# Shifted copies on GpSimd, and more slots for the ring that holds them, in a four-layer attention kernel

## The chip, the cores and the metric

The kernel runs on one core of a Trainium2 chip. The metric is the device time of one execution in microseconds (us); lower is better. The core has a matrix engine (TensorE, PE in the profile, with its weight loads as PEld), a vector engine (VectorE, DVE), an activation engine (ScalarE, ACT), a general engine (GpSimd, POOL) and a queue that issues DMAs (SyncE, SP). Each works through its own list of instructions in order and waits for the others by semaphores.

## The reference

Four layers run one after the other on x of 2048 tokens by 512 columns, with 32 heads of 16. Layers 0 and 2 (kind A) attend causally within four segments of 512 tokens and add a memory term; layers 1 and 3 (kind B) are plain attention of all 2048 tokens.

```python
def _A_ref(x, wq, wk, wv, wo, beta):
    ...
    for s in range(N):                       # N = 4 segments of 512 tokens
        qs, ks, vs = (q[:, :, s].copy(), k[:, :, s].copy(), v[:, :, s].copy())
        logits = jnp.einsum('bhqd,bhkd->bhqk', qs, ks) * scale + mask
        p = _softmax(logits, axis=-1)
        a_dot = jnp.einsum('bhqk,bhkd->bhqd', p, vs)
        pq = phi(qs)
        num = jnp.einsum('bhld,bhde->bhle', pq, M)
        den = jnp.einsum('bhld,bhd->bhl', pq, z)[..., None] + 1e-06
        o = g * (num / den) + (1.0 - g) * a_dot
        outs.append(o)
        pk = phi(ks)
        M = M + jnp.einsum('bhld,bhle->bhde', pk, vs)
        z = z + jnp.einsum('bhld->bhd', pk)
    ...

def _B_ref(x, wqkv, wo):
    ...
    scores = jnp.einsum('bhqd,bhkd->bhqk', q, k) * Dh ** (-0.5)
    p = _softmax(scores, axis=-1)
    o = jnp.einsum('bhqk,bhkd->bhqd', p, v)
    return (lambda x, *d: x.transpose(*d))(o, 0, 2, 1, 3).reshape(B, S, D) @ wo

x = A_x
x = x + _A_ref(_layernorm(x, axis=-1), A_wq, A_wk, A_wv, A_wo, A_beta)
x = x + _B_ref(_layernorm(x, axis=-1), B_wqkv, B_wo)
x = x + _A_ref(_layernorm(x, axis=-1), A_wq, A_wk, A_wv, A_wo, A_beta)
x = x + _B_ref(_layernorm(x, axis=-1), B_wqkv, B_wo)
```

## The kernel before

**A program that plans itself.** The Python code keeps a list of instructions for each engine (class `Sched`) and, for each, an estimate of when it ends (`estimate`): `sc.t["dve"]` is the time at which VectorE, by this estimate, is done with all that it was given so far. An instruction is given a duration `ns` and a spacing `gap`, which is `ns - 85` unless it is said otherwise. Where and in what order work is put into the lists is decided by these estimates while the program is built; on the chip the lists then run as they are, held together by semaphores alone. Every tensor region has a `Buf` that remembers its last writer and its readers, from which the waits are made.

**Banks of logits.** A group is four heads (every second one of a chunk of 128 columns) with one segment of 512 queries. Its logits are made in banks, each of one head, 128 keys and 512 queries, with a 32-row matmul (`ps<-qm,KB` in the profile; `qm` is the group's masked copy of the queries, made on GpSimd or VectorE at L1161). A group of kind B has 64 banks. A unit (`unit`) is up to three banks next to each other in PSUM. ScalarE takes their exponential in one instruction (L1244, `pT<-ps`, of 1536, 1024 or fewer columns), and the result is multiplied with V by four 128-column matmuls per bank (`ps<-VB,pT`). In layers of kind A, GpSimd blanks the future keys in `pT` (L1259). When all banks of a group are in, VectorE divides by the row sums (`finish`, L1333 and L1345).

**VectorE's exponential.** Some banks of kind B don't go to ScalarE. VectorE reads the logits from PSUM, scales them and stores them as 16-bit integers whose bits, taken as bfloat16, are a coarse exponential (`dx_first`, L900, of one bank or two). Then it makes three copies, each with another constant added (`EXP_D` = 0, 22, 54, 92; `dx_chain`, L946), and the matmuls with V add up all four (`ps<-VB,dxw` and so on): sixteen matmuls for a bank in place of four. Two banks make a pair. A pair takes four slots of a ring, one for the read and one for each copy; a slot holds 1024 columns, in two halves. A slot is free again when the matmuls that read it have been put in the list.

**The ring.** It has nine slots in a tensor of its own (`dxw`), and six more in the second half of KA, QA and VA, which only the first A layer uses. These are added to the list of free slots (`dx_bufs`) in `dx_widen` when the last segment of layer 0 is through; `wide` is set then. They appear in the profile under the names of the tensors that they lie in: `KA<-ps`, `QA<-dxw`, `ps<-VB,VA` are all work of the ring.

**When a pair is begun.** In `compose`, each unit asks `dx_room`, which says no when few banks are left, when a pair is to be begun and fewer than `DXS` = 4 slots are free, or when VectorE's planned time, with 350 ns for each copy that is still to be made, is over `DQ` = 2200 ns past the unit's start. `dx_find` gives no more than a third of a group's banks to VectorE. The copies are two tasks of the background (`task_dx`), taken one step at a time between units, within a credit of VectorE's time.

**Which engine copies.** In `dx_chain` a copy goes to GpSimd when `POOL_ON` isn't zero and, by the plan, GpSimd would be done with it (`POOL_T` after the later of GpSimd's planned time and the end of the pair's read) before VectorE's planned time plus `POOL_ON`. In the kernel before, `POOL_ON` is 0, and all copies are VectorE's.

Of the kernel before, what the change touches and what calls it, by code (L numbers as in the profile page):

```python
# [3 lines left out]
dt = mybir.dt  # L4
# [73 lines left out]
class Sched:  # L78
# [40 lines left out]
    def add(self, eng, fn, reads=(), writes=(), deps=(), name="", banks=(), ns=300, gap=None, tile=None):  # L119
# [53 lines left out]
        for (bk, mode, alloc) in banks:  # L173
            if mode == "w":
                bk.writes.append(op)
            else:
                bk.reads[eng] = op
                bk.last_read_any = op
# [75 lines left out]
class Builder:  # L254
# [10 lines left out]
    CR_A, CR_B, CR_W, CR_LOW, CARRY, CARRY_W, REST, NEAR, SLACK = 1300, 1500, 1400, 2200, 0, 0, 14, 10, 300  # L265
    ALT3, ALT5, GAP, AHEAD, PE_B, PE_A, PE_LOW, LOW, PAIRS, TAKEN, PAIRS2 = 2, 4, 3, 500, 4, 3, 4, 24, 60, 3, 1
    NKS = 6
    DX_T, POOL_T, POOL_ON = 430, 1150, 0
    DQN, TAKEN_N, REST_N, NEAR_N, NEAR_W = 600, 3, 14, 100, 24
    DQ, DXS, PVN, PVLATE, PVWAIT = 2200, 4, 4, 600, 0  # L270
    DMA_STEPS, DMA_LATE = 2, 300
# [9 lines left out]
    def alloc(self):  # L281
        nc = self.nc
        bf, f32 = dt.bfloat16, dt.float32
        sb = nc.alloc_sbuf_tensor
        self.x = sb("x", [P, NT, D], bf)
        self.xn = sb("xn", [P, 2, D], bf)
        self.xT = sb("xT", [P, 2, NCH, 512], bf)
        self.wA = sb("wA", [P, NCH, 3 * D], bf)
        self.wB = sb("wB", [P, NCH, 3 * D], bf)
        self.woA = sb("woA", [P, NCH, D], bf)  # L290
        self.woB = sb("woB", [P, NCH, D], bf)
        self.KB = sb("KB", [P, self.NKS, NCH, 512], bf)
        self.VB = sb("VB", [P, self.NKS, 4, 544], bf)
        self.QB = sb("QB", [P, 4, NCH, 512], bf)
        self.KA = sb("KA", [P, 2, NCH, 512], bf)
        self.QA = sb("QA", [P, 2, NCH, 512], bf)
        self.VA = sb("VA", [P, 2, 4, 544], bf)
        self.phk = sb("phk", [P, 4, 512], bf)
        self.phq = sb("phq", [P, NCH, 512], bf)
        self.amem = sb("amem", [P, 2, 4, 128], bf)  # L300
        self.oT = sb("oT", [P, 2, NCH, 512], bf)
        self.ob = sb("ob", [P, 2, 4, 128], bf)
        self.rd = sb("rd", [P, 2, 16], f32)
        self.pT = sb("pT", [P, self.NPU, 3, 512], bf)
        self.qm = sb("qm", [P, 4, 512], bf)
        self.dxw = sb("dxw", [P, self.NDX, 1024], dt.uint16)
        self.ident = sb("ident", [P, P], bf)
        self.zero = sb("zero", [P, P], bf)
        self.hmask = sb("hmask", [P, 8], f32)
        self.lnst = sb("lnst", [P, 2, 4, 8], f32)  # L310
        self.lnw = sb("lnw", [P, 2, 4, 4], f32)
        self.bet = sb("bet", [P, H], bf)
        self.gtok = sb("gtok", [P, H], f32)
        self.gout = sb("gout", [P, H], f32)
        self.M = sb("M", [P, NCH, 8, 17], f32)
        self.Mn = sb("Mn", [P, NCH, 8, 16], bf)
        self.Mz = sb("Mz", [P, NCH, 8], bf)
        self.rg = sb("rg", [P, 1, 4, H], f32)
        self.ps = nc.alloc_psum_tensor("ps", [P, 4096], f32)
        self.psb = self.ps[:, :].bitcast(bf)  # L320
        self.sems = {e: nc.alloc_semaphore(f"ev_{e}") for e in ENGS}
        self.tsems = [[nc.alloc_semaphore(f"tr{i}"), 0, None] for i in range(8)]
        self.dsems = [nc.alloc_semaphore(f"dma{i}") for i in range(24)]

        B = Buf
        n2 = lambda nm, a, b: [[B(f"{nm}{i}_{j}") for j in range(b)] for i in range(a)]
        n1 = lambda nm, a: [B(f"{nm}{i}") for i in range(a)]
        self.b_x = n1("x", NT)
        self.b_xn = n1("xn", 2)
        self.b_xT = n2("xT", 2, 4)  # L330
        self.b_wA = n1("wA", 3)
        self.b_wB = n1("wB", 1)
        self.b_woA, self.b_woB = B("woA"), B("woB")
        self.b_KB = n2("KB", self.NKS, NCH)
        self.b_VB = n2("VB", self.NKS, 4)
        self.b_QB = n2("QB", 4, NCH)
        self.b_KA = n2("KA", 2, NCH)
        self.b_QA = n2("QA", 2, NCH)
        self.b_VA = n2("VA", 2, 4)
        self.b_phk = n1("phk", 4)  # L340
        self.b_phkc = n1("phkc", NCH)
        self.b_phq = n1("phq", NCH)
        self.b_amem = n1("amem", 2)
        self.b_oT = n2("oT", 2, NCH)
        self.b_ob = n2("ob", 2, 2)
        self.b_rd = n1("rd", 2)
        self.b_pT = n1("pT", self.NPU * 3)
        self.b_qm = n1("qm", 4)
        self.b_dxw = n2("dxw", self.NDX + 6, 2)
        self.b_last = n1("last", 2)  # L350
        self.b_zero = B("zero")
        self.b_ident, self.b_hm = B("ident"), B("hm")
        self.b_lnst = n2("lnst", 2, 4)
        self.b_lnw = n1("lnw", 2)
        self.b_bet, self.b_g, self.b_gout = B("bet"), B("g"), B("gout")
        self.b_M, self.b_Mn, self.b_Mz = n1("M", 2), B("Mn"), B("Mz")
        self.b_rg = n1("rg", 1)
        self.banks = [Bank(i) for i in range(8)]
        self.nalloc = 0
        self.rr = {}  # L360
# [345 lines left out]
    def task_B(self, L, s):  # L706
        ks = self.kslot(L, s)
        need = [("x", L, s)]
        if L == 3:
            need.append(("attn", 1, s))  # L710
            if s == 0:
                need.append(("attn", 1, 0))
            if s >= 2:
                need.append(("attn", 1, 3))
        yield need, 0, 0
        k = yield from self.ln_part(L, s)
        yield ["xT"], 0, 0
        slot = self.take_xT()
        yield from self.ln_tiles(L, s, k, slot)
        yield [("dma", ("xT", L, s))], 0, 0  # L720
        for c in range(NCH):
            yield from self.proj_fm(self.wB, self.b_wB[0], 512, slot, c, self.KB[:, ks, c, :], self.b_KB[ks][c])
            self.flags.add(("K", L, s, c))
            yield from self.proj_fm(self.wB, self.b_wB[0], 0, slot, c, self.QB[:, s, c, :], self.b_QB[s][c])
            self.flags.add(("Q", L, s, c))
            if c == 0:
                for ti in range(4):
                    vt = self.VB[:, ks, ti, :]
                    bv = self.b_VB[ks][ti]
                    on = vt.rearrange("p (h f) -> p h f", f=17)[:, :, 16:17]  # L730
                    self.op("pool", (lambda on: lambda e: e.memset(on, 1.0))(on), writes=[bv])
                    yield from self.proj_tm(self.wB, self.b_wB[0], 1024, slot, ti, self.v_evac(vt, bv))
                self.flags.add(("V", L, s))
        self.give_xT(slot)

    def task_out(self, L, s):
        isA = L % 2 == 0
# [111 lines left out]
    def pending(self):  # L849
        return any(t not in self.dx_tasks and self.met([n for n in t["next"][0] if n[0] != "at"]) for t in self.tasks)  # L850

    def dx_space(self, i):

        if i < self.NDX:
            return self.dxw[:, i, :]
        j = i - self.NDX
        if j < 4:
            a = (self.KA, self.QA)[j // 2][:, 1, :, :].rearrange("p a b -> p (a b)")
        else:
            a = self.VA[:, 1, :, :].rearrange("p a b -> p (a b)")  # L860
        return a[:, 1024 * (j % 2):1024 * (j % 2) + 1024].bitcast(dt.uint16)

    def dx_writes(self, i, h):

        if i < self.NDX or (i, h) in self.dx_seen:
            return [self.b_dxw[i][h]]
        self.dx_seen.add((i, h))
        return [self.b_dxw[i][h]] + (self.b_KA, self.b_QA, self.b_VA)[(i - self.NDX) // 2][1]

    def dx_widen(self):  # L870

        if not self.wide and ("attn", 0, 3) in self.flags and ("mem", 0, 3) in self.flags:
            self.wide = True
            self.dx_bufs += range(self.NDX, self.NDX + 6)

    def aslot(self, L, s):
        return 0 if L else s % 2
# [526 lines left out]
    def attention(self):  # L1404
# [3 lines left out]
        self.sel, self.pvq, self.deferred, self.qm_free = [], [], [], [0, 1, 2, 3]  # L1408
        self.qm_late = []

        self.dx_use, self.dx_bufs = [0] * (self.NDX + 6), list(range(self.NDX))
        self.dx_build, self.dx_pairs, self.dx_now, self.dxq, self.dx_own = [], [], [[], []], [], []
        self.dx_seen, self.wide, self.dx_todo = set(), False, 0
        self.dx_step = self.bank_step = -9
# [10 lines left out]
        n = 0  # L1425
# [95 lines left out]
```

## Time and profile before

| | |
|---|---|
| median of 3 runs | 1959.38 us (1953.49 to 1965.37) |
| the profiled execution | 1956.4 us, of which the span from the first to the last instruction is 1954.7 us |
| ScalarE busy | 1828.6 us (94%), of which L1244, the exponentials, 1799.6 us |
| TensorE busy | 1761.4 us (90%) |
| VectorE busy | 1500.5 us (77%) |
| GpSimd busy | 285.0 us (15%), of which L1259 209.6 us and the masks of L1161 68.1 us |
| VectorE's copies of 1024 columns, dxw to dxw | 437, mean 428 ns |
| VectorE's reads of two banks, into dxw | 156, mean 1221 ns |
| VectorE's reads of one bank, into dxw | 209, mean 687 ns |

The page lists an engine's busy time, its share of the span, and for each group of instructions (line, engine, operation, what it writes and reads, how many) the busy time, the mean of one, and the idle time of the engine before it with what ended it. A busy TensorE isn't one at its peak, since ends of matmuls are modelled; starts of its weight loads are the better clock. GpSimd's durations hold time in which it waits for memory as well as work.

### The profile page before, as it was taken

Reading aid. Unit: us, or ns where it says so; the run is one execution under the profiler, and the core shown is the slowest. Engines: PE = TensorE matmul, PEld = TensorE weight load, DVE = VectorE, ACT = ScalarE, POOL = GpSimd, SP = SyncE. Lnnn points to the kernel's source line nnn. Section 1 sums busy time; section 2 is a strip of 40 time slices with the busy share of each in tenths; the row PEclk is TensorE's granted clock in tenths of the full one; section 3 lists DMA queues with packets and bytes.
Section 4 is the critical chain, followed back from the end, with each engine's and each line's share of the span. In section 5 each row is a group of like instructions: output and inputs, shape, how many; then the busy total and the mean of one; then the engine's idle time right before and its main releaser. Section 6 shows DMA issues by size and latency. Waiting matters only on the chain.

```text
span 1954.7 us, 79981 instructions
## 1 busy us (share of the span) xinstructions
PE 1761.4 (90%) x35997; PEld 1135.1 (58%) x36232; DVE 1500.5 (77%) x3154; ACT 1828.6 (94%) x1641; POOL 285.0 (15%) x642
## 2 busy tenths in 40 slices
PE   7788888889979999899997999889899999999998
PEld 4344444556646666466664666445666666666665
DVE  5656566788858887688876888577888888888886
ACT  6789988899999999899998999988999999999998
POOL 3432153010050000500005000320100000000000
PEclk9999999999999999899999999999999999999999
DMA  4110111000011000100001001000000000000000
GB/s 152 27 36 18 29 21 31 14 11 11 10 27 16 3 8 14 34 9 14 8 14 37 5 6 24 18 8 13 11 16 9 6 17 6 6 6 16 6 6 16
DMA packets 101016, 35.96 MB, mean 18 GB/s; under 512 B 93505, under 2 KB 100161, under 8 KB 100673
## 3 DMA queue, kind: packets, MB, share of 16 engines
q1 hardware_dynamic: 100672, 30.83, 8.1%
q8 instruction: 283, 4.64, 1.0%
q14 instruction: 61, 0.49, 0.1%
HBM read 6.30 MB, written 2.10 MB: 4 GB/s over the span
## 4 chain that ended last, share of the span: by engine, by line
PE 37%; ACT 36%; DVE 12%; issue 12%; DMA 2%; POOL 1%; SPq 0%; ACTq 0%; DVEq 0%; POOLq 0%
PE ps L389 37%; ACT pT L1244 36%; DVE dxw L900 2%; DVE dxw L946 1%; DMA xT<-xn 1%; DVE ob L1345 1%; POOL pT L1259 1%; ACT amem L584 1%; DVE VA L900 0%; DVE QA L900 0%; DVE rd L1333 0%; DVE QA L946 0%; DVE KA L946 0%; DVE VA L946 0%; DVE KB L416 0%
## 5 line engine op out<-in xcount | busy, mean ns | idle before, releaser
L1244 ACT ACTIVATE pT<-ps 128x1536 bf16<-128x1536 f32 (+3 forms) x1600 | 1799.6, 1260 | 100.6 <-PE ps L389 80.4
L389 PEld LDWEIGHTS ps<-VB,pT 128*128 128x128 bf16 x12872 | 427.9, 96 | 324.6 <-issue 233.3
L389 PE MATMUL ps<-qm,KB 32*128 32x512 bf16 x4096 | 524.4, 387 | 63.2 <-ACT pT L1244 45.8
L389 PE MATMUL ps<-VB,pT 128*128 128x51 bf16 (+1 forms) x12872 | 551.7, 187 | 28.9 <-DVE ob L1345 16.4
L900 DVE TENSOR_SCALAR dxw<-ps 128x512 uint16<-128x512 f32 (+1 forms) x365 | 333.4, 915 | 85.3 <-PE ps L389 80.9
L389 PE MATMUL ps<-VB,dxw 128*128 128x51 bf16 (+1 forms) x8520 | 362.1, 186 | 0.9 <-DVE dxw L946 0.9
L1259 POOL TENSOR_SCALAR_AFFINE_SELECT pT<-pT 128x256 bf16<-128x256 bf16 (+2 forms) x513 | 209.6, 427 | 552.6 <-ACT pT L1244 543.3
L389 PEld LDWEIGHTS ps<-VB,dxw 128*128 128x128 bf16 x8520 | 282.3, 96 | 1.4 <-DVE dxw L946 1.1
L389 PEld LDWEIGHTS ps<-qm,KB 32*128 32x128 bf16 x4096 | 130.0, 91 | 179.0 <-ACT pT L1244 97.7
L1161 POOL TENSOR_SCALAR qm<-QB,par 128x512 bf16<-128x512 bf16 x86 | 68.1, 794 | 1020.2 <-PE ps L389 895.1
L946 DVE TENSOR_SCALAR dxw<-dxw 128x1024 uint16<-128x1024 uint16 (+1 forms) x454 | 182.8, 423 | 3.3 <-PE ps L389 0.7
L389 PE MATMUL ps<-qm,KA 32*128 32x512 bf16 (+3 forms) x1024 | 105.0, 312 | 36.0 <-ACT pT L1244 31.4
L389 PE MATMUL ps<-VA,pT 128*128 128x51 bf16 (+1 forms) x2560 | 114.9, 190 | 22.8 <-DVE ob L1345 14.4
L389 PEld LDWEIGHTS ps<-VA,pT 128*128 128x128 bf16 x2560 | 87.1, 98 | 79.1 <-POOL pT L1259 43.5
L389 PEld LDWEIGHTS ps<-qm,KA 32*128 32x128 bf16 x1024 | 30.0, 92 | 112.5 <-ACT pT L1244 77.8
L900 DVE TENSOR_SCALAR KA<-ps 128x512 uint16<-128x512 f32 (+1 forms) x91 | 80.2, 882 | 18.8 <-PE ps L389 17.6
L389 PE MATMUL ps<-VB,QA 128*128 128x51 bf16 (+1 forms) x1848 | 90.0, 186 | 0.0
L900 DVE TENSOR_SCALAR VA<-ps 128x512 uint16<-128x512 f32 (+1 forms) x83 | 75.2, 906 | 18.7 <-PE ps L389 17.6
L389 PE MATMUL ps<-VB,KA 128*128 128x51 bf16 (+1 forms) x1844 | 89.0, 185 | 0.1
L389 PE MATMUL ps<-VB,VA 128*128 128x51 bf16 (+1 forms) x1836 | 87.3, 185 | 0.0
L900 DVE TENSOR_SCALAR QA<-ps 128x512 uint16<-128x512 f32 (+1 forms) x82 | 74.5, 909 | 14.5 <-PE ps L389 13.8
L1333 DVE RECIPROCAL rd<-ps 128x16 f32<-128x16 f32 x112 | 28.3, 253 | 69.6 <-PE ps L389 69.1
(125 smaller groups left out, 1540.0 us busy)
## 6 DMA issues: line engine op xcount, KB each, us to landing
out_dram<-x SPq DMA_DIRECT2D x8, 256.0 KB, 2.2
x<-in_A_x_dram SPq DMA_DIRECT2D x3, 512.0 KB, 9.0
wB<-in_B_wqkv_dram SPq DMA_DIRECT2D x1, 1536.0 KB, 13.0
oT<-ob SPq DMA_TRANSPOSE x63, 2.4
xT<-xn SPq DMA_TRANSPOSE x60, 2.5
x<-in_A_x_dram SPq DMA_DIRECT2D x4, 128.0 KB, 2.2
wA<-in_A_wk_dram SPq DMA_DIRECT2D x1, 512.0 KB, 4.7
wA<-in_A_wq_dram SPq DMA_DIRECT2D x1, 512.0 KB, 5.7
```

The source lines that it names most:

```text
L389: self.sc.add("pe", lambda e: e.matmul(out, lhsT, rhs, start=start, stop=stop, skip_group_check=True), reads=reads, banks=[(bank, "w", all ...
L584: self.op("act", lambda e: e.activation(et, src, ACT.Exp), reads=bsrc, writes=self.b_amem, ns=1023, gap=915)
L900: self.sc.add("dve", lambda e: e.tensor_scalar(d, o, SCALE * LOG2E * 128, EXP_C, op0=ALU.mult, op1=ALU.add), writes=[w for j in range(k) f ...
L946: self.op(eng, (lambda o, d: lambda e: e.tensor_scalar(o, w, d, None, op0=ALU.add))(o, d), reads=bw, writes=wr, ns=ns, name="dxs")
L1161: self.op(eng, (lambda m, q, col: lambda e: e.tensor_scalar(m, q, col, 0.0, op0=ALU.mult, op1=ALU.add))(m, q, col), reads=[bq, self.b_par] ...
L1244: self.sc.add("act", (lambda dst, src: lambda e: e.activation(dst, src, ACT.Exp, scale=SCALE))(dst, src), writes=self.b_pT[slot * 3 + i:sl ...
L1259: self.op("pool", (lambda blk, pat: lambda e: e.affine_select(blk, blk, pattern=pat, compare_op=ALU.is_ge, fill=0.0, base=0, channel_multi ...
L1333: self.op("dve", lambda e: e.reciprocal(rd, src[:, :, 16]), reads=bsrc, writes=[br], bank=bk, alloc=al, ns=253)
L1345: self.op("dve", lambda e: e.tensor_tensor(ob, src[:, :, 0:16], rb, ALU.mult), reads=[br] + bsrc, writes=[self.b_ob[oi][g.e]], bank=bk, al ...
```

## The change

Three things are edited.

- `POOL_T` goes from 1150 to 1800 and `POOL_ON` from 0 to 300: the condition in `dx_chain`, which stood unused, now sends a copy of a pair to GpSimd when its planned end there, 1800 ns after the later of GpSimd's planned time and the read's end, is before VectorE's planned time plus 300 ns.
- `dx_areas` lists 36 areas of 1024 columns, each with the flags that must be set before it is used: the six of before; six in `wA` when the projections of layer 2 are done; twelve in the first halves of KA, QA and VA and in `woA`, `phk` and `phq` when layer 2 is through; eight in KB and VB of two segments when the first query segment of layer 3 is through; four in `xT` when the last input of layer 3 has been projected.
- `dx_widen` opens each area by itself when its flags are set, `dx_space` and `dx_writes` look the area up, and `task_B` sets the flag `("in", L, s)` that the `xT` areas need.

```diff
-    DX_T, POOL_T, POOL_ON = 430, 1150, 0
+    DX_T, POOL_T, POOL_ON = 430, 1800, 300
...
-        self.b_dxw = n2("dxw", self.NDX + 6, 2)
+        self.b_dxw = n2("dxw", self.NDX + self.NAREA, 2)
...
         self.give_xT(slot)
+        self.flags.add(("in", L, s))
...
+    def dx_areas(self):
+        areas = []
+
+        def add(t, n, bufs, *need):
+            for j in range(n):
+                areas.append((t[:, 1024 * j:1024 * j + 1024].bitcast(dt.uint16), bufs(j), need))
+        flat = lambda t: t.rearrange("p a b -> p (a b)")
+        first = (("attn", 0, 3), ("mem", 0, 3))
+        add(flat(self.KA[:, 1, :, :]), 2, lambda j: self.b_KA[1], *first)
+        add(flat(self.QA[:, 1, :, :]), 2, lambda j: self.b_QA[1], *first)
+        add(flat(self.VA[:, 1, :, :]), 2, lambda j: self.b_VA[1], *first)
+        add(flat(self.wA[:, :, :]), 6, lambda j: self.b_wA, ("proj", 2, 3))
+        last = (("attn", 2, 3), ("mem", 2, 3), ("op", 2, 3))
+        add(flat(self.KA[:, 0, :, :]), 2, lambda j: self.b_KA[0], *last)
+        add(flat(self.QA[:, 0, :, :]), 2, lambda j: self.b_QA[0], *last)
+        add(flat(self.VA[:, 0, :, :]), 2, lambda j: self.b_VA[0], *last)
+        add(flat(self.woA[:, :, :]), 2, lambda j: [self.b_woA], *last)
+        add(flat(self.phk[:, :, :]), 2, lambda j: self.b_phk + self.b_phkc, *last)
+        add(flat(self.phq[:, :, :]), 2, lambda j: self.b_phq, *last)
+        for ks in (2, 3):
+            add(flat(self.KB[:, ks, :, :]), 2, lambda j: self.b_KB[ks], ("attn", 3, 0))
+            add(flat(self.VB[:, ks, :, :]), 2, lambda j: self.b_VB[ks], ("attn", 3, 0))
+        for k in range(2):
+            add(flat(self.xT[:, k, :, :]), 2, lambda j: self.b_xT[k], ("in", 3, 3))
+        return areas
...
     def dx_space(self, i):
-        if i < self.NDX:
-            return self.dxw[:, i, :]
...
+        return self.dxw[:, i, :] if i < self.NDX else self.areas[i - self.NDX][0]
...
-        return [self.b_dxw[i][h]] + (self.b_KA, self.b_QA, self.b_VA)[(i - self.NDX) // 2][1]
+        return [self.b_dxw[i][h]] + self.areas[i - self.NDX][1]
...
     def dx_widen(self):
-        if not self.wide and ("attn", 0, 3) in self.flags and ("mem", 0, 3) in self.flags:
-            self.wide = True
-            self.dx_bufs += range(self.NDX, self.NDX + 6)
+        for n, (_, _, need) in enumerate(self.areas[:self.XDX]):
+            if n not in self.dx_open and all(f in self.flags for f in need):
+                self.dx_open.add(n)
+                self.dx_bufs.append(self.NDX + n)
+                self.wide = True
+
+    NAREA, XDX = 38, 99
```

More of the change, by code (lines that the diff above doesn't have):

```diff
@@ L850, in pending @@
         return any(t not in self.dx_tasks and self.met([n for n in t["next"][0] if n[0] != "at"]) for t in self.tasks)
-    def dx_space(self, i):
-        if i < self.NDX:
-            return self.dxw[:, i, :]
[L856 to L861, printed above, removed]
+    def dx_areas(self):
[22 more added lines that the diff above has]
+        return areas
+    def dx_space(self, i):
+        return self.dxw[:, i, :] if i < self.NDX else self.areas[i - self.NDX][0]
     def dx_writes(self, i, h):
@@ L1409, in attention @@
         self.qm_late = []
-        self.dx_use, self.dx_bufs = [0] * (self.NDX + 6), list(range(self.NDX))
+        self.dx_use, self.dx_bufs = [0] * (self.NDX + self.NAREA), list(range(self.NDX))
+        self.areas, self.dx_open = self.dx_areas(), set()
         self.dx_build, self.dx_pairs, self.dx_now, self.dxq, self.dx_own = [], [], [[], []], [], []
```

## The prediction

> **What bounds the kernel now.** I read the engines' sums by stage first, then the waits of the last stage, then single instructions. The change acts from about 340 us on, where L900 first writes into KA, QA and VA. I call 340 to 1370 us the middle stage and 1370 to 1955 the last one; the last A layer's matmuls are over by 1303. The two stages by window (columns: stretch, its length, then busy time and count of PE, PEld, DVE, ACT, POOL, the granted clock, DMA share, GB/s):
> ```profile
> 340.00:1370.00 1030.00, 932.81 (x18905) 601.95 (x19046) 804.74 (x1751) 965.07 (x872) 148.15 (x323) 0.98 0.08 14
> 1370.00:1955.00 585.00, 548.73 (x13241) 385.09 (x13273) 491.27 (x892) 573.79 (x492) 20.51 (x27) 0.99 0.06 10
> ```
> In the last stage ScalarE works 573.8 of 585 us, TensorE 548.7, VectorE 491.3, GpSimd 20.5. ScalarE sets the time, TensorE stands 25 us behind it and VectorE 82. In the middle stage ScalarE is again the longest, with 65 of 1030 us idle. The waits of the last stage (who waited for whom, us, times, longest):
> ```profile
> PEld ps L389 <- ACT pT L1244: 44.3, 94, 0.9
> DVE dxw L900 <- PE ps L389: 33.7, 24, 2.6
> ...
> DVE rd L1333 <- PE ps L389: 21.5, 15, 10.0
> ```
> TensorE has some 45 us in which it waits for ScalarE. VectorE's idle time is waiting for TensorE: for the next logits, and 21.5 us for a finished sum. No wait on a shifted copy is of that size: the chip's VectorE keeps up with the plan.
>
> **What a bank costs on each engine**, from the last stage's timeline, where VectorE goes read, copy, copy, copy without a gap:
> ```profile
> 1650.54 1.22 DVE L900 TENSOR_SCALAR dxw<-ps 128x1024 uint16<-128x1024 f32 x1
> 1651.80 0.43 DVE L946 TENSOR_SCALAR dxw<-dxw 128x1024 uint16<-128x1024 uint16 x1
> 1652.14 0.42 DVE L946 TENSOR_SCALAR KA<-dxw 128x1024 uint16<-128x1024 uint16 x1
> 1652.47 0.42 DVE L946 TENSOR_SCALAR dxw<-dxw 128x1024 uint16<-128x1024 uint16 x1
> 1652.81 1.22 DVE L900 TENSOR_SCALAR VA<-ps 128x1024 uint16<-128x1024 f32 x1
> ```
> By starts a copy takes 0.34 us and a pair of banks 2.27. ScalarE does 283 activations of three banks and 206 of two in this stage, 1261 banks in 573.8 us: 0.455 each. A bank on VectorE has four copies to multiply instead of one, so 12 more weight loads and matmuls; 16 such loads take 0.48 us at 1650.57 and one takes 0.096, so a further one costs 0.026, and 12 cost 0.31. **One more pair on VectorE: ScalarE -0.91, TensorE +0.62, VectorE +2.27.**
>
> **The change, part by part.**
> *How many copies GpSimd gets.* It gets one when the pair's read ended, by the plan, over 1.5 us before VectorE's planned time (1800 - 300), and is then booked 1.8 us. Slots named KA, QA or VA tell how old the source of a copy is: in the middle stage 187 of 294 were over 1.5 us old (64%), in the last 7 of 243. The three copies of a pair age together and GpSimd can take one per 1.8 us, so one in three: 709 copies x 0.64 / 3 = 151. In the last stage the order above gives ages of 0.03, 0.37 and 0.71 us: none, as it stands. With more slots a second pair can wait there; at most one of each three copies then, 597 / 3 = 199; I take half, 100. Together 250; the ends are 0, and 454 + 325 = 779 (all old ones, and one per 1.8 us in the last stage).
>
> *What a moved copy costs.* No copy on GpSimd is in this trace. The nearest row is its mask, 692 ns for 512 columns; L1259's 520 and 292 ns for 384 and 128 columns give a fixed part of 0.18, so 1024 columns make 1.2 us. VectorE gains 0.34. Against that, VectorE's copies wait while GpSimd works. Two masks, and VectorE's copies beside them:
> ```profile
> 1615.52 1.21 POOL L1161 TENSOR_SCALAR qm<-QB,par 128x512 bf16<-128x512 bf16 x1 [22.22 <-DVE dxw L900]
> ```
> ```profile
> 1615.83 0.42 DVE L946 TENSOR_SCALAR dxw<-dxw 128x1024 uint16<-128x1024 uint16 x1
> 1616.17 0.84 DVE L946 TENSOR_SCALAR VA<-dxw 128x1024 uint16<-128x1024 uint16 x1
> 1616.93 1.21 DVE L900 TENSOR_SCALAR dxw<-ps 128x1024 uint16<-128x1024 f32 x1
> ```
> ```profile
> 1704.14 0.69 POOL L1161 TENSOR_SCALAR qm<-QB,par 128x512 bf16<-128x512 bf16 x1 [20.42 <-PE ps L389]
> ```
> ```profile
> 1704.02 1.23 DVE L900 TENSOR_SCALAR dxw<-ps 128x1024 uint16<-128x1024 f32 x1
> 1705.28 0.76 DVE L946 TENSOR_SCALAR dxw<-dxw 128x1024 uint16<-128x1024 uint16 x2
> ```
> The first mask, released behind a read as a moved copy would be, waited for two copies (1.21 instead of 0.69 us) and then held up the third (0.84 instead of 0.42). The second lay under a read of PSUM and cost nothing. Of the 23 masks after 1400 us, 13 stretched a copy, by 0.43 on average: 0.24 per mask. For 1.2 us instead of 0.69 I scale to **0.42 per moved copy**; the ends are 0 (the second row) and 1.2 - 0.27 = 0.93 (the first: its mask of 0.69 cost 0.42). So a moved copy leaves VectorE 0.08 us worse, between 0.34 better and 0.59 worse.
>
> The Trainium skill (GPSIMD Engine Reference, Elementwise, side-by-side cycle accounting) gives GpSimd's best loop as 1.8 cycles per element, 769 ns for 512. The mask's 692 ns is below that, so I keep the row; by the page a copy would be an estimated 1.54 us, the stall 0.54 and the loss 0.20.
>
> *What the plan does with it.* It counts 350 ns less for VectorE per moved copy and no stall, and fills that with reads: 250 x 0.35 = 87 us at 1140 + 3 x 350 = 2190 ns a pair are 40 pairs, 24 of them in the middle stage, 16 in the last.
>
> *The slots.* Counting reads and copies as they open slots, and matmuls as they use them up, 20 of the 30 half slots are in use on average in the last stage, with peaks of 24 to 26; a new pair needs four free slots, so it is the ring that refuses pairs there. The new slots open at about 1244 (wA), 1303 (the A layer's), 1353 (xT) and 1419 us (KB, VB), so they matter in the last stage alone. VectorE's 94 idle us there less the 21.5 for finished sums hold at most 32 pairs; I take 24, with 0 and 32 as ends. A first write to an opened slot also waits for the old readers, matmuls that ended before it opened: nothing, and if the plan is ahead of the chip, one wait of under a microsecond per slot.
>
> *Queues.* No DMA is added or moved. On GpSimd's queue the masks (one per some 21 us in the last stage) and L1259's selects now stand behind moved copies, up to 1.2 us plus a wait, and logits stand behind the masks. I cost it at nothing: the last stage's masks are made about a group ahead; without that cover it is 23 x 1.2 = 28 us. The end above nothing goes into the range.
>
> *The sum.* Middle stage, 24 pairs and 151 moved copies: ScalarE 965 - 22 = 943, TensorE 933 + 15 = 948, VectorE 805 + 54 + 12 = 871. The longest falls by 17; since 65 us there already go to waits, I take half, -9. Last stage, 40 pairs and 100 moved copies: ScalarE 574 - 36 = 538, TensorE 549 + 25 = 574, VectorE 491 + 91 + 8 = 590, and 22 that it must wait for finished sums: 612, **VectorE becomes the bound, +27**. Together +18. The profiled execution took 1956.4 us (span 1954.7 and 1.7 around it), 3.0 below the median shown: 1974.4, or 1977 from the median. I say 1975.
>
> **Rivals.**
> *Faster: the copies slip under the reads.* If a moved copy waits for two copies and then runs under the next 1.25 us read, it costs nothing; one copy fewer between reads makes just this order. Then VectorE in the last stage needs 491 + 91 - 34 + 22 = 570, TensorE's 574 is the bound: -11; the middle stage gives between -9 and its full -17: 1956.4 - 24 = 1932. It decides below a stall of 0.15 us per moved copy (491 + 91 - 34 + 22 + 15 = 585). For it: 10 of 23 masks cost nothing. Against it: the other 13.
> *Much slower: the stall is the whole operation.* At 0.93 VectorE in the last stage comes to 491 + 91 + 59 + 22 = 663, +78, and in the middle stage to 805 + 54 + 89 = 948, level with TensorE, no gain: 2034. For it: a moved copy is released by its own read, right where the other copies start.
> *It hardly does what it says.* If the last stage's copies stay under 1.5 us old and the reads are refused for another reason, little moves there and the middle stage gains and loses alike: 1957, within 8. For it: 7 of 243.
>
> **Chances and range.** Forecast 0.38 (its own range 1965 to 2000), under the reads 0.35, whole operation 0.12, hardly anything 0.15. About 0.5% (10 us round 1959.4) is what a measurement of this kernel can tell. Slower: 0.34 of the forecast and the 0.12, 0.46; same: 0.15 and the forecast's other 0.04, 0.19; faster 0.35. From 1930, just below the faster case, to 2025, short of the worst, leaves out a quarter of the first and over half of the third, under 0.2.
>
> **What would show it.** Right: some 250 copies of 1.2 us and more on GpSimd; VectorE's own copies well above 0.43 on average; some 60 more pairs in L900; ScalarE's share down from 94%, with PE waiting for dxw. Wrong: moved copies in the hundreds with VectorE's copies still near 0.42 (the faster rival); GpSimd's copies near 1.8 us of pure work; fewer than 100 moved; a last stage in which TensorE, not VectorE, ends last although ScalarE has idle time.

## The result, and the profile after

The changed kernel takes 2189.41 us (median of 4 runs, 2186.22 to 2197.84) against 1960.5 for the kernel before: a ratio of 1.1173, 95% interval 1.1147 to 1.1199. It is 229 us slower, where 15 to 18 were forecast. The way was right, which the prediction gave a chance of 0.46; the size is off by a factor of more than ten, and 2189 lies far outside the range.

The first part of the page after, and the groups of the copies (now L972), from its fifth part:

```profile
PE 1919.3 (88%) x36852; PEld 1209.7 (55%) x36852; DVE 1669.8 (76%) x2885; ACT 1838.6 (84%) x1640; POOL 1459.3 (67%) x1062
...
L972 POOL TENSOR_SCALAR dxw<-dxw 128x1024 uint16<-128x1024 uint16 x76 | 218.2, 2873 | 99.4 <-DVE dxw L926 92.1
...
L972 DVE TENSOR_SCALAR dxw<-dxw 128x1024 uint16<-128x1024 uint16 (+1 forms) x253 | 135.5, 560 | 4.9 <-POOL dxw L972 1.7
```

GpSimd goes from 15% to 67%. A copy there takes 2873 ns, not the 1200 of the prediction's estimate nor the 1800 that the plan books; a copy on VectorE takes 560 on average in this group, 581 without its 18 copies of 512 columns, instead of 428. ScalarE's busy time has hardly moved (1838.6 against 1828.6 us), its share has: it now waits. The same stages by window, the last one cut at the end of the kernel before:

```profile
340.00:1370.00 1030.00, 921.28 (x17687) 580.02 (x17686) 762.19 (x1420) 900.00 (x802) 590.33 (x438) 0.93 0.08 13
1370.00:1955.00 585.00, 509.98 (x10788) 341.63 (x10787) 502.63 (x702) 467.66 (x405) 526.61 (x249) 0.91 0.04 9
1955.00:2190.00 235.00, 200.47 (x4450) 139.75 (x4450) 198.20 (x253) 179.99 (x154) 220.24 (x83) 0.91 0.04 9
```

The loss begins before the last stage. By 1370 us ScalarE and VectorE have done 2902 banks (counted as 512 columns each), against 3077 in the kernel before; at the rate of before in the middle stage (2485 banks in 1030 us) that is an estimated 73 of the 229 us. GpSimd is busy there for 590 us instead of 148, and ScalarE for 900 instead of 965.

In the 235 us behind the end of the kernel before, GpSimd is busy for 220, the longest of all engines, and ScalarE for 180. Who waits, from the last stage's waits, first one row of before, then after:

```profile
ACT pT L1244 <- PE ps L389: 4.0, 12, 0.6
```
```profile
ACT pT L1270 <- PE ps L389: 155.9, 198, 4.5
PEld ps L389 <- issue: 141.0, 522, 0.8
PEld ps L389 <- DVE ob L1371: 31.8, 24, 2.6
```

ScalarE waited 4.0 us for TensorE in this stage before; now it is 155.9, in a stage of 819 us instead of 585. What TensorE waits for is spread over many rows, of VectorE's sums, reads and copies and of GpSimd's copies. The rhythm shows the cause better. One pair in the timeline after (start and length in us, engine, line, operation, what it writes and reads), first VectorE, then GpSimd:

```profile
1703.15 1.21 DVE L926 TENSOR_SCALAR dxw<-ps 128x1024 uint16<-128x1024 f32 x1
1704.40 0.56 DVE L972 TENSOR_SCALAR dxw<-dxw 128x1024 uint16<-128x1024 uint16 x1
1704.88 1.25 DVE L972 TENSOR_SCALAR dxw<-VA 128x1024 uint16<-128x1024 uint16 x1
1706.05 1.21 DVE L926 TENSOR_SCALAR KB<-ps 128x1024 uint16<-128x1024 f32 x1
```
```profile
1701.86 2.82 POOL L972 TENSOR_SCALAR wA<-KA 128x1024 uint16<-128x1024 uint16 x1
1704.65 2.93 POOL L972 TENSOR_SCALAR dxw<-dxw 128x1024 uint16<-128x1024 uint16 x1
1707.55 2.93 POOL L972 TENSOR_SCALAR QA<-VA 128x1024 uint16<-128x1024 uint16 x1
```

From read to read it is 2.90 us (1703.15 to 1706.05), against 2.27 before, although VectorE makes one copy fewer. GpSimd has no gap between its copies. VectorE has none either: its second copy takes 1.25 us where 0.42 would do. In these pairs the two engines have locked into one period, the length of a GpSimd copy: VectorE's reads before and behind, at 1700.25 and 1708.95, stand at the same 2.90 us.

### The profile page after: what moved, and what is told of

It reads as the page before. It is cut to its first block, busy times and chain, and to the rows that moved or that the text cites. A ratio compares the mean times of both kernels' runs of the same rounds, so it can differ in the third digit from the quotient of the medians.

```text
span 2189.4 us, 82012 instructions
## 1 busy us (share of the span) xinstructions
PE 1919.3 (88%) x36852; PEld 1209.7 (55%) x36852; DVE 1669.8 (76%) x2885; ACT 1838.6 (84%) x1640; POOL 1459.3 (67%) x1062
## 4 chain that ended last, share of the span: by engine, by line
PE 22%; DVE 17%; POOL 10%; issue 5%; ACT 4%; ACTq 0%; POOLq 0%; DVEq 0%
PE ps L389 22%; ACT pT L1270 4%; POOL dxw L972 3%; DVE dxw L972 2%; POOL VA L972 2%; DVE dxw L926 1%; POOL QA L972 1%; POOL wA L972 1%; DVE KA L926 1%; DVE wA L972 1%; DVE VA L972 1%; POOL KA L972 1%; DVE KA L972 1%; DVE QA L972 1%; DVE ob L1371 1%
## 5 line engine op out<-in xcount | busy, mean ns | idle before, releaser
L1270 ACT ACTIVATE pT<-ps 128x1024 bf16<-128x1024 f32 (+4 forms) x1598 | 1808.5, 1202 | 324.1 <-PE ps L389 299.0
L389 PE MATMUL ps<-qm,KB 32*128 32x512 bf16 x4096 | 582.8, 407 | 62.0 <-ACT pT L1270 23.2
L926 DVE TENSOR_SCALAR dxw<-ps 128x512 uint16<-128x512 f32 (+1 forms) x298 | 246.9, 833 | 72.5 <-PE ps L389 68.8
L389 PE MATMUL ps<-VB,dxw 128*128 128x51 bf16 (+1 forms) x5980 | 266.5, 189 | 25.8 <-POOL dxw L972 24.5
L972 POOL TENSOR_SCALAR dxw<-dxw 128x1024 uint16<-128x1024 uint16 x76 | 218.2, 2873 | 99.4 <-DVE dxw L926 92.1
L389 PEld LDWEIGHTS ps<-VB,dxw 128*128 128x128 bf16 x5980 | 208.3, 98 | 28.5 <-POOL dxw L972 26.8
L972 DVE TENSOR_SCALAR dxw<-dxw 128x1024 uint16<-128x1024 uint16 (+1 forms) x253 | 135.5, 560 | 4.9 <-POOL dxw L972 1.7
L389 PE MATMUL ps<-qm,KA 32*128 32x128 bf16 (+3 forms) x1024 | 105.8, 317 | 33.0 <-ACT pT L1270 28.8
L972 POOL TENSOR_SCALAR VA<-dxw 128x1024 uint16<-128x1024 uint16 x22 | 62.7, 2848 | 48.8 <-DVE dxw L926 47.5
L972 POOL TENSOR_SCALAR QA<-dxw 128x1024 uint16<-128x1024 uint16 x27 | 76.8, 2845 | 24.2 <-DVE dxw L926 22.7
```

Source lines behind the costliest of these rows:

```text
L389: self.sc.add("pe", lambda e: e.matmul(out, lhsT, rhs, start=start, stop=stop, skip_group_check=True), reads=reads, banks=[(bank, "w", all ...
L926: self.sc.add("dve", lambda e: e.tensor_scalar(d, o, SCALE * LOG2E * 128, EXP_C, op0=ALU.mult, op1=ALU.add), writes=[w for j in range(k) f ...
L972: self.op(eng, (lambda o, d: lambda e: e.tensor_scalar(o, w, d, None, op0=ALU.add))(o, d), reads=bw, writes=wr, ns=ns, name="dxs")
L1270: self.sc.add("act", (lambda dst, src: lambda e: e.activation(dst, src, ACT.Exp, scale=SCALE))(dst, src), writes=self.b_pT[slot * 3 + i:sl ...
```

## The experiments

Three causes were possible: GpSimd's own length (late copies, and GpSimd as the bound), VectorE's copies held up, and the fuller plan that the new slots allow. The first four runs begin to separate them. Each ratio is against runs of the kernel before that were made with it, with medians of 1956.06 to 1956.37 us.

**The slots alone.**

```diff
-    DX_T, POOL_T, POOL_ON = 430, 1800, 300
+    DX_T, POOL_T, POOL_ON = 430, 1800, 0
```

> The change with POOL_ON = 0: all new slots, no copy on GpSimd. If GpSimd's copies cost the 230 us (by their own length, or by holding up VectorE's copies): within 15 us of the kernel before, 1940 to 1975, VectorE some 24 pairs more in the last stage, its copies 0.42 us. If the fuller plan that the slots allow overloads VectorE and TensorE by itself: over 2000.

1967.88 us, ratio 1.0063 (1.0041 to 1.0085). VectorE takes 923 banks instead of 878, its copies stay at 0.42. The slots aren't the loss; they cost 12 us by themselves. TensorE's weight loads wait 19.2 us for VectorE's last operations of a group in the last stage (4.5 before), which is followed up below.

**The GpSimd copies alone.**

```diff
-    NAREA, XDX = 38, 99
+    NAREA, XDX = 38, 6
```

> The change with the six areas of before alone (XDX = 6): GpSimd copies, no new slots. If the copies in the middle stage cost what the trace after shows there (181 banks fewer done by 1370 us, some 75 us) and the last stage needs the new slots to have old copies at all: 2000 to 2060, some 165 to 200 copies on GpSimd, few after 1400 us. If the new slots carry the loss: under 1975.

2060.8 us, ratio 1.0536 (1.0507 to 1.0565), just past the upper end of what was expected. 210 copies go to GpSimd, 165 of them in the middle stage as in the kernel after, but only 42 in the last one instead of 250. The new slots are what lets copies grow old there. By 1370 us 2894 banks are done, as few as in the kernel after, so the middle stage's loss comes from the GpSimd copies alone. The two parts by themselves cost 104 and 12 us; together they cost 229.

**Booked at its real length.**

```diff
-    DX_T, POOL_T, POOL_ON = 430, 1800, 300
+    DX_T, POOL_T, POOL_ON = 430, 2850, 300
...
-                eng, ns = "pool", self.POOL_T if len(ents) == 2 else 700
+                eng, ns = "pool", self.POOL_T if len(ents) == 2 else 1500
```

> The change with a GpSimd copy booked at 2850 ns (1500 for 512 columns) in place of 1800 (700). If the loss is that GpSimd takes longer than the plan books, so that TensorE and VectorE wait for its copies: those waits go, 1940 to 1985, GpSimd under 80% busy in the last stage. If the loss is that each moved copy holds up VectorE's copies by some 0.6 us: 200 to 300 moved copies still cost 50 us and more, over 2010.

2091.67 us, ratio 1.0702 (1.0666 to 1.0737). TensorE's waits for moved copies are gone from the waits, 325 copies are moved instead of 418, GpSimd is 77% busy in the last stage (551.71 of 714 us), and it is still 135 us slower than before. So the wrong booking can be a part of the loss, not most of it; how large a part is not shown, since fewer copies move.

**The same copies as bfloat16.**

```diff
+            if eng == "pool":
+                ob, wb, m = o.bitcast(dt.bfloat16), w.bitcast(dt.bfloat16), 2.0 ** (d / 128)
+                self.op(eng, (lambda ob, wb, m: lambda e: e.tensor_scalar(ob, wb, m, 0.0, op0=ALU.mult, op1=ALU.add))(ob, wb, m),
+                        reads=bw, writes=wr, ns=ns, name="dxs")
+            else:
...
```

> The change with GpSimd's copies made as a bfloat16 multiplication of the same bits by 2^(d/128) in place of an integer addition, so these copies hold other values. If the 16-bit integer type makes GpSimd slow: 1.2 us a copy, as the mask's row scales, and a time near that of the kernel before, 1930 to 1990. If a copy takes 2.8 us because VectorE's copies hold GpSimd up: 2.5 us or more still, and over 2100.

The copy took 1.10 to 1.15 us on average, as the prediction had scaled it from the mask: it is the 16-bit integer addition that is slow on GpSimd. (Type and operation were changed together; the slower form has one operation, the faster one two.) But the time is 2070.08 us, ratio 1.0589 (1.0564 to 1.0615), and TensorE's waits show no moved copy. With GpSimd fast enough, 102 us over the slots alone remain. VectorE's copies are longer by 153 us in all, counted over 0.42 us for each, which is 0.38 per moved copy. The last stage by window, and a stretch of the timeline:

```profile
1370.00:2072.00 702.00, 640.54 (x14452) 445.87 (x14476) 613.99 (x875) 598.14 (x513) 305.57 (x283) 0.93 0.05 9
```
```profile
1699.35 1.21 DVE L926 TENSOR_SCALAR KB<-ps 128x1024 uint16<-128x1024 f32 x1
1700.48 0.41 DVE L976 TENSOR_SCALAR VB<-VB 128x1024 uint16<-128x1024 uint16 x1
1700.81 1.26 DVE L976 TENSOR_SCALAR VB<-KB 128x1024 uint16<-128x1024 uint16 x1
1702.00 1.21 DVE L926 TENSOR_SCALAR xT<-ps 128x1024 uint16<-128x1024 f32 x1
1703.24 0.43 DVE L976 TENSOR_SCALAR xT<-xT 128x1024 uint16<-128x1024 uint16 x1
```
```profile
1700.64 1.15 POOL L974 TENSOR_SCALAR xT<-KB 128x1024 bf16<-128x1024 bf16 x1 [1.82 <-DVE KB L926]
1701.88 1.10 POOL L974 TENSOR_SCALAR KB<-KB 128x1024 bf16<-128x1024 bf16 x1
```

Both cases of the prediction stand side by side. The first GpSimd copy holds up VectorE's second one (1.26 us, done 0.28 after GpSimd); the second lies under a read and costs nothing. The average, 0.38, is near the 0.42 that was forecast. But the 102 us aren't VectorE's added work: it is busy 1576.6 us here and 1540.6 with the slots alone, 36 more.

**The two operations by themselves.** Behind the end of the kernel before, GpSimd and VectorE copies on nothing but each other.

```diff
+        for k in range(3):
+            self.sc.add("pool", add(S(1), S(0)), reads=bx, writes=[self.b_dxw[1][0], self.b_dxw[1][1], z])
...
+            for k in range(3):
+                self.sc.add("pool", f(cast(S(1)), cast(S(0))), reads=[y] if not k else [], writes=[self.b_dxw[1][0], self.b_dxw[1][1], z])
+            for k in range(24):
+                self.sc.add("dve", add(S(3), S(2)), writes=[self.b_dxw[3][0], self.b_dxw[3][1]] + ([y] if k == 23 else []))
```

> The kernel before, with GpSimd and VectorE operations added behind its end: GpSimd copies of 1024 and 512 columns alone, as integers and as bfloat16, then three of each kind beside 24 VectorE copies that depend on nothing. If the integer type is what is slow: alone 2.8 and 1.5 us as integers, 1.05 and 0.6 as bfloat16. If VectorE's copies make them long: about equal alone. If a VectorE copy that meets a GpSimd copy waits to its end: with the integer copies one of them in 2.8 us; if it waits some 0.85 us at most, as in the trace after: several.

GpSimd alone (groups of the probe by form: busy us, mean ns):

```profile
L1478 POOL TENSOR_SCALAR dxw<-dxw 128x1024 uint16<-128x1024 uint16 x3 | 8.3, 2769 | 92.7 <-ACT x L813 92.6
L1478 POOL TENSOR_SCALAR dxw<-dxw 128x512 uint16<-128x512 uint16 x3 | 4.5, 1487 | 0.2
L1479 POOL TENSOR_SCALAR dxw<-dxw 128x1024 bf16<-128x1024 bf16 x3 | 3.1, 1044 | 0.2
```

With VectorE idle the integer copy takes 2769 ns and the bfloat16 one 1044. Contention adds little to GpSimd's own time. Then both at once, VectorE's copies beside one integer copy that runs from 1980.52 to 1983.53:

```profile
1980.94 1.14 DVE L1478 TENSOR_SCALAR dxw<-dxw 128x1024 uint16<-128x1024 uint16 x1
1982.11 0.43 DVE L1478 TENSOR_SCALAR dxw<-dxw 128x1024 uint16<-128x1024 uint16 x1
1982.57 1.24 DVE L1478 TENSOR_SCALAR dxw<-dxw 128x1024 uint16<-128x1024 uint16 x1
```

One copy waits, one gets through undisturbed, one waits again to the end. Alone one takes 0.43, so an integer copy costs VectorE 0.71 + 0.81 = 1.52 us when it has nothing but copies to do; beside the two integer copies that follow it is the same. Beside three bfloat16 copies:

```profile
L1478 DVE TENSOR_SCALAR dxw<-dxw 128x1024 uint16<-128x1024 uint16 x3 | 3.4, 1144 | 0.1
```

That is 0.72 us per GpSimd copy. Against that stands the 0.34 us that a moved copy saves.

**Nothing moved, GpSimd merely kept at work.** The kernel before, its order on VectorE, ScalarE and TensorE unchanged, with one GpSimd copy per pair added from 1244 us on, into `wA`, which nobody reads by then; and the same with integer copies at every second pair.

```diff
+        if ("proj", 2, 3) in self.flags:
+            sc = self.wA[:, :, :].rearrange("p a b -> p (a b)")[:, 0:n]
+            self.sc.add("pool", lambda e: e.tensor_scalar(sc, w.bitcast(dt.bfloat16), 1.125, 0.0, op0=ALU.mult, op1=ALU.add),
+                        reads=bw, writes=self.b_wA, ns=1, gap=0, name="spare")
```

> The kernel before with nothing moved, and one GpSimd bfloat16 copy added per pair from 1244 us on, into memory that nobody reads (wA); the order of VectorE, ScalarE and TensorE is that of before. If holding up VectorE's copies is enough for a loss: some 200 copies of 1.1 us, VectorE's copies 0.4 us longer for each, 2000 to 2050. If VectorE's idle time (94 us in the last stage) takes these in, and the loss comes from the fuller plan alone: under 1975.

2107.53 us, ratio 1.0749 (1.0698 to 1.0800): beyond what was expected. 216 copies that nobody waits for (no wait on one is in its waits) cost 151 us, 0.70 each. Its last stage by window, and its waits there:

```profile
1370.00:2110.00 740.00, 631.13 (x13506) 423.98 (x13539) 657.69 (x913) 607.41 (x503) 284.42 (x234) 0.93 0.05 8
```
```profile
ACT pT L1247 <- PE ps L389: 123.5, 184, 1.7
PEld ps L389 <- DVE dxw L900: 67.8, 88, 1.4
```

VectorE's copies in this stage are longer by 166 us in all, again over 0.42 us each. The stage takes 740 us for 1692 banks, 724 at the 1656 banks of before: 139 us longer. So 84% of the lost VectorE time reaches the end, although VectorE had 94 us idle there before and is 89% busy now. Over the whole run VectorE, with the same instructions, is busy 1665.0 us instead of 1500.5, and 151 of these 164.5 us are in the time. TensorE waits for VectorE's reads of PSUM (L900), which free the bank that the next logits go to, and ScalarE waits for TensorE. In this kernel's chain of waits over that stage, VectorE's copies are 45% and its reads 30%.

> As the run with idle bfloat16 copies, with integer copies and one per two pairs. If the whole of the copy's 2.8 us held VectorE up: as much VectorE time lost as there or more, 1990 to 2050. If it is some 0.85 us and a little per copy, whatever the copy's length: about half of that run's loss, 1970 to 2005.

2026.87 us, ratio 1.0339 (1.0285 to 1.0392), a little above the 2005 of the case that came: by time it would fit the other case (1990 to 2050), but that one needs as much VectorE time lost as with the bfloat16 copies, and it is about half. 108 copies cost 71 us, 0.66 each. An integer copy takes VectorE about as much as a bfloat16 one here (89 us of longer copies for 100 in the last stage, 0.89 each, against 0.82), although it is 2.7 times as long.

**Is it the refill?** In the next two a copy on GpSimd also counts as VectorE's planned time.

```diff
                 eng, ns = "pool", self.POOL_T if len(ents) == 2 else 700
+                self.sc.t["dve"] += 350 if len(ents) == 2 else 248
```

> The run with bfloat16 copies, but a copy on GpSimd also counts its 350 ns (248 for 512 columns) of VectorE's planned time, so that the plan sees no relief to fill with pairs (the copies hold other values, as there). If that run's 114 us are the fuller plan, the copy's own gain and stall being about equal (0.34 against 0.42 us): near the slots alone, 1955 to 1990. If the stalls themselves cost it: 2030 and more.

> The change, with a copy on GpSimd also counting 350 ns (248) of VectorE's planned time: integer copies, no refill. If the refill is the larger part of the loss: under 2020. If the integer copy's stalls (1.5 us at most by the probe, 0.6 to 0.9 seen) are: 2040 to 2130, GpSimd still 60% busy and more in the last stage.

2042.92 us (ratio 1.0444, 1.0406 to 1.0482) with bfloat16 copies, 2377.2 us (1.2155, 1.2118 to 1.2191) with integer ones. The edit did more than was meant: VectorE's planned time runs ahead, so more copies pass the condition: 551 in each of the two runs, where the kernel after moves 418. But VectorE's banks stay at 922, as with the slots alone (923) and hardly under the kernel after (932): the plan never filled the relief with many more pairs. The refill falls as a cause of any size. The run with bfloat16 copies lies where it was expected if the stalls themselves cost the time (2030 and more). The one with integer copies lies far above both of its cases (under 2020, and 2040 to 2130), because so many more copies went to GpSimd. Per moved copy, over the slots alone, the bfloat16 copy costs 0.14 us here and the integer copy 0.74; GpSimd is then 908.23 of 1006 us busy in the last stage and sets the time.

**A shorter lead.** What the slots alone lose is TensorE waiting at a group's end, behind VectorE's planned lead; so the lead was cut, GpSimd's copies left out. First with the slots:

```diff
-    DVE_FIN, DX_FIN = 600, 2500
+    DVE_FIN, DX_FIN = 600, 1000
...
-    DQ, DXS, PVN, PVLATE, PVWAIT = 2200, 4, 4, 600, 0
+    DQ, DXS, PVN, PVLATE, PVWAIT = 1600, 4, 4, 600, 0
```

> The change without GpSimd's copies (POOL_ON = 0), VectorE's planned lead cut from 2200 to 1600 ns (DQ) and from 2500 to 1000 ns ahead of a group's end (DX_FIN). If the 0.6% that the slots alone lose is TensorE waiting for VectorE's last operations of a group (some 30 us there, 5 before): these waits under 12 us and a time of 1935 to 1955. If the added pairs themselves are too many: still 1960 or more.

> The kernel before with the shorter planned lead alone (DQ 1600, DX_FIN 1000), no new slots. If the 0.2% that slots and short lead gain together comes from the lead: 1945 to 1958 here too. If it needs the slots: 1958 to 1975, since the last stage is then short of slots and lead.

> The new slots without GpSimd's copies, the planned lead cut further (DQ 1200, DX_FIN 400). If TensorE's waits for VectorE's last operations of a group still cost (31 us with DQ 1600 and DX_FIN 1000): 1935 to 1950. If VectorE now gets too few banks: 1955 to 1980.

With the slots 1953.21 us, ratio 0.9976 (0.9954 to 0.9999): the time that was expected, but the waits at the group's end are hardly shorter (17.6 us of weight loads). The lead without the slots: 1959.62 us, 1.0023 (1.0005 to 1.0041). With the slots and the lead cut further (DQ 1200, DX_FIN 400): **1931.59 us, ratio 0.9882 (0.9852 to 0.9911), less than both kernels**. Its stages by window:

```profile
340.00:1370.00 1030.00, 950.70 (x19181) 602.29 (x19181) 797.13 (x1644) 982.66 (x871) 151.73 (x332) 0.99 0.09 14
1370.00:1931.00 561.00, 533.94 (x13097) 379.32 (x13092) 500.20 (x912) 541.88 (x470) 20.49 (x24) 0.99 0.04 10
```

ScalarE works 982.66 us of the middle stage, 18 more than before, so less of it is idle; TensorE's weight loads wait 13.0 us for VectorE's last operations of a group. VectorE's banks are 876, as many as before. The gain comes from less waiting, and it lies in the middle stage: by 1370 us 3139 banks are done, 62 more than before, an estimated 26 us at the rate of before, which is the whole gain. Of these 62, some 23 are done by 1244 us, before any new slot is used, so a part of the gain needs no slots. With the first of the shorter leads the slots are worth 6 us (1953.21 against 1959.62). What they are worth with the second was not tried: it was not run without them, nor were the two numbers one by one.

## Why the prediction came out so

- **What bounds the kernel, and the price of a pair:** ScalarE at the longest, 2.27 us a pair on VectorE: nothing in the runs speaks against these. The reading of VectorE's idle time as room for more work does fall, see the sum.
- **How many copies move:** 151 in the middle stage was right (165). In the last one 100 were forecast and 250 came: with the new slots one copy of each pair moves, the end of which I had taken half.
- **The copy's length, the first step that failed:** the term that was most mis-sized. 1.2 us was scaled from a bfloat16 mask; as bfloat16 the copy takes 1.04 alone, as the 16-bit integer that it is 2.77, and 2.86 in the kernel after. The rival with the long operation went by the stall alone and did not make GpSimd itself a bound; in the added 235 us it is the longest. Between the losses with bfloat16 and with integer copies lie 115 us, half of the whole.
- **The stall:** 0.42 per moved copy was right for a copy of the length forecast (0.38 with bfloat16). In the kernel after it is 0.59: VectorE's copies are 248 us longer, over 0.42 each, for 418.
- **The net of the copy and the sum, the second step that failed:** "leaves VectorE 0.08 us worse" held with bfloat16 copies (0.38 against the 0.34 saved), yet about 100 us followed from it; with integer copies it is 0.25 worse. The sum takes a stage to last as long as its longest engine is busy. In the last stage VectorE was to fill its idle time and then set the end with 22 us of waits; with bfloat16 copies it kept 88 us idle there (613.99 of 702 busy). In the middle stage -9 was forecast, on ScalarE's time alone; the kernel after ends it an estimated 73 us behind, with no engine busy for more than 921 of 1030 us. Added GpSimd work with nothing moved shows the same: 84% of VectorE's lost time in the last stage reaches the end.
- **The refill:** 40 pairs were forecast on top of the slots' 24. The slots gave 22 (923 banks against 878), the relief some 5 more.
- **The slots:** a small gain was implied, a loss of 0.6% came. With the lead of 1600 they gain 6 us; the 1.2% gained with the lead of 1200 can't be put down to them.
- **The faster rival** needed a stall under 0.15 us. In the runs it was 0.3 or more with every kind of copy (the least with bfloat16 copies and no refill).
- **The slower rival** had GpSimd hold VectorE up and came to 2034, with an operation of 1.2 us. It was nearest, and still 155 us short: it too adds up busy time.

Of the 229 us the slots bring 12, bfloat16 copies in GpSimd's place 102 more, and the integer type's length 115 more. How the last part divides between GpSimd as the bound, copies that come later than booked and longer stalls stays open: with the right booking 135 us remain, but fewer copies move. Open too is how the 102 us come about with only 36 us more work on VectorE. Late reads that keep TensorE and then ScalarE waiting are the likely way, which the idle copies show for a loss of VectorE time; that they do it here is argued.

## What to carry to other kernels

Before work goes to another engine, measure the very operation there, with its number type: a neighbouring row of the same engine was wrong by a factor of 2.3. Work that VectorE copies must wait for is not free even when nobody reads its result; price it by what it holds up: here 0.34 us saved stands against 0.7 lost. An engine's idle share need not be slack where it stands in a loop with two others: here a read that comes late frees its bank late, and the next unit's logits, then ScalarE, wait for it.

## What the runs showed of the hardware that wasn't expected

A GpSimd tensor_scalar that adds to 16-bit integers takes 2769 ns for 1024 columns, one that multiplies and adds in bfloat16 1044; for 512 it is 1487 and 617. The best-loop figure of the Trainium skill that the prediction weighed (GPSIMD Engine Reference, Elementwise, side-by-side cycle accounting) gives an estimated 1.54 us for 1024 columns; that lies between the two measured times and is neither.

The Trainium skill (SBUF — State Buffer, Who interferes with whom) has the port that the two engines share held for a whole instruction. For the bfloat16 copy the probe agrees: VectorE's copy ends 0.28 us after GpSimd's. For the integer copy it doesn't: within its 3.0 us two VectorE copies are held up by 0.71 and 0.81 us, and one between them runs in its usual 0.43. The measurement decides. That the port is free for a moment in between is the likely reading; no run shows the port itself.

The granted clock of TensorE was 0.983 before, 0.93 in the kernel after and 0.887 in the slowest run, of 2377 us. It doesn't follow the time alone: it was 0.967 in the profiled run of 2086 us (booked at 2850) and 0.953 in that of 2074 us (bfloat16 copies). What share of the loss it makes was not tried.
